# A gated attention and token-MLP block: attention by token halves with pre-added products, a bf16 softmax, weights copied by DMA, and attention summed into the MLP's PSUM

## The chip, the cores and the metric

The kernel runs on one core of one Trainium2 chip, written directly against the engines' instruction queues. Time is the device time of one execution in microseconds (us). A profile is one such execution, and its span runs from the first to the last instruction. Engines: PE (matmul), DVE (vector), ACT (activations), POOL (GpSimd) and SP (which issues DMAs). PSUM is the accumulator memory, which these kernels declare as eight banks of 512 fp32 per partition.

Each execution also lists the mean TensorE clock that was granted, as a share of full speed. The kept traces don't show it for the first 4 to 11 us: their clock records begin that late or are missing, and the profile prints 1.00 where it has none.

## The reference

`x` is 2048 tokens by 512. Two branches are mixed by a gate.

```python
g = sigmoid((x * gate_w).sum(-1))                 # one number per token
# A: 32 heads of 16, each token attends to 8 tokens: itself and those 2, 4, ... 14 before it
q, k, v = split(x @ wqkv)
logits = einsum("bhsd,bhswd->bhsw", q, k[s - 2*w]) * 0.25      # masked where s - 2*w < 0
o = einsum("bhsw,bhswd->bhsd", softmax(logits), v[s - 2*w])
a = o @ wo
# B: an MLP over the tokens
u = gelu(einsum("bsd,sf->bdf", layernorm(x), w1) + b1)         # 2048 -> 1792
b = transpose(einsum("bdf,fs->bds", u, w2) + b2)               # 1792 -> 2048
out = g * a + (1 - g) * b
```

The projections are 192 matmuls of 128x128 by 512, the MLP 448 and `wo` 64. The sliding-window attention has no large matmul: DVE multiplies q with shifted k, and attention weights with shifted v, element by element. PE only sums these products across partitions.

## The kernel before

The kernel names operations with what they read and write. At build time a list scheduler orders each engine's queue, and then every queue runs in order. The parts that the change touches, cut:

```python
# scores: a product of q with 4 shifted k per (half of the window, dl); PE sums each over 4 partitions
for wh in range(2):
    for dl in range(4):
        A("dve", f_qkm(wh, dl, buf), ...)         # tensor_tensor 128x8192 bf16
        A("pe", f_qkr(wh, dl, buf), ...)          # 16 tiled matmuls, 32 output rows each
    A("act", ... LOG[:, 4*wh:4*wh+4] = copy(ps[:, 4:8]) ...)       # fp32
# softmax in fp32: max, subtract, exp, sum, reciprocal, multiply (512 columns)
# 16 DMAs, issued by SP, copy V into the layout of the weights (V3)
# values: product of 4 shifted v with the weights, three adds of 128x2048, then PE sums
for t in range(4):
    for wh in range(2):
        A("dve", f_avm(t, wh, buf), ...)          # tensor_tensor 128x8192 bf16
        ...                                       # ava, avb, avc: 128x2048 adds
        A("pe", f_ws(t, wh, buf), ...)            # 16 tiled matmuls
    A("act", ... OT[:, t] = copy(ps[:, 4:8]) ...)
# MLP, then out = g * (OT @ WO) + T1
for i in range(NST):
    ... 14 matmuls; ACT: T1[:, i] = (1-g) * psum + c2
    A("pe", f_wo(i), ...)                         # 4 matmuls into a bank of their own
    A("dve", ... OUTS = psum * g + T1[:, i] ...)
    sch.dma("sp", ... outv[:, i] = OUTS ...)
```

## Time and profile before

| | before |
|---|---|
| median time of the first three executions | 187.16 us (186.28 to 188.75) |
| span of the profiled execution | 183.8 us |
| PE / DVE / ACT busy | 171.3 / 151.5 / 76.5 us |
| first score product on DVE, first MLP matmul on PE | 25.8, 65.8 us |

The head of the profile's page, and the two lines of its chain of waits. The chain is followed back from the last instruction. The lines give shares of the span by engine, then by source line (L791: second MLP layer; L752: first; L618: score products).

```profile
span 183.8 us, 2564 instructions
...
PE 171.3 (93%) x1071; PEld 80.5 (44%) x1091; DVE 151.5 (82%) x139; ACT 76.5 (42%) x98; POOL 0.9 (0%) x8
...
PE 70%; DVE 22%; ACT 3%; issue 2%; DMA 2%
PE ps L791 26%; PE ps L752 26%; DVE arena L618 18%; PE ps L808 7%; PE ps L584 6%; DVE arena L549 2%; DMA arena<-in_A_x_dram 2%; PE ps L510 2%; PE ps L709 1%; ACT arena L529 1%; ACT L543 1%; PE ps L625 1%; DVE arena L820 0%; ACT arena L765 0
```

PE is busy 93% of the span and makes up 70% of the chain. The costliest groups show each operation with shapes, count, total busy time and mean ns of one:

```profile
L752 PE MATMUL ps<-arena 128*128 128x512 bf16 x219 | 48.5, 379 | 0.4 <-issue 0.2
L584 PE MATMUL ps<-arena 128*128 128x512 bf16 x185 | 44.4, 391 | 2.7 <-ACT arena L529 1.6 <-DVE arena L539 0.5 <-issue 0.3
L701 DVE TENSOR_TENSOR arena<-arena 128x8192 bf16<-128x8192 bf16 x8 | 35.2, 4420 | 0.1
L618 DVE TENSOR_TENSOR arena<-arena 128x8192 bf16<-128x8192 bf16 x8 | 34.9, 4419 | 0.0
...
L625 PE MATMUL ps<-arena 128*32 128x512 bf16 x128 | 8.2, 382 | 0.7 <-DVE arena L618 0.7
...
L709 PE MATMUL ps<-arena 32*32 32x512 bf16 x128 | 3.2, 384 | 0.0
```

A DVE product of 8192 elements takes 4.42 us. The 379 ns of a matmul run from its start to its end, and matmuls overlap. What one costs in a stream comes from the timeline, where a GELU leaves every 3.455 us per 16 matmuls: 0.216 us each.

The timeline (start, duration, engine, line, operation; in brackets the idle time just before and what ended it) fixes three events: the first score products, the first MLP matmul, and DVE's idle time near the end, because only output tiles are left for it.

```profile
25.78 4.42 DVE L618 TENSOR_TENSOR arena<-arena 128x8192 bf16<-128x8192 bf16 x1
...
65.77 1.47 PE L752 MATMUL ps<-arena 128*128 128x512 bf16 x6
...
160.38 3.34 DVE L820 SCALAR_TENSOR_TENSOR arena<-ps,arena 128x512 bf16<-128x512 f32 x4 [7.93 <-PE ps L808]
```

### The profile page before, as it was taken

How to read it: one execution, taken by the hardware profiler on the slowest of the kernel's cores; microseconds unless marked ns; L12 is line 12 of the kernel's file. 1: busy time of each engine (PE TensorE's matmuls, PEld its weight loads, DVE VectorE, ACT ScalarE, POOL GpSimd, SP SyncE). 2: the span in 40 equal slices, each digit the busy share in tenths (PEclk: the TensorE clock that was granted, in tenths of full speed). 3: DMA queues.
4: the chain of work that ended last, by engine and by line, in shares of the span. 5: the costliest groups of instructions: out<-in, count | busy, mean ns of one | idle time of the engine just before them, and what ended most of it. 6: DMA issues, size and time to landing. Idle time of an engine off the chain costs nothing.

```text
span 183.8 us, 2564 instructions
## 1 busy us (share of the span) xinstructions
PE 171.3 (93%) x1071; PEld 80.5 (44%) x1091; DVE 151.5 (82%) x139; ACT 76.5 (42%) x98; POOL 0.9 (0%) x8
## 2 busy tenths in 40 slices
PE   0789999999999989999999999899999999999993
PEld 0455554454564334444434444344444444444441
DVE  0867759999999999699999999999999991056524
ACT  2267686565677373962111251161225226110110
POOL 1000000000000000000000000000000000000000
PEclk9999999999999999999999999999999999999999
DMA  5999990000000079999999200007625742033113
GB/s 181 334 343 262 250 229 5 0 4 2 2 4 0 0 227 173 175 257 214 290 290 291 71 0 0 4 0 200 181 65 157 199 139 65 0 114 114 51 63 114
DMA packets 37870, 23.29 MB, mean 127 GB/s; under 512 B 996, under 2 KB 37860, under 8 KB 37860
## 3 DMA queue, kind: packets, MB, share of 16 engines
q1 hardware_dynamic: 37860, 23.14, 50.6%
q8 instruction: 8, 0.13, 0.3%
q14 instruction: 2, 0.02, 0.0%
HBM read 18.88 MB, written 2.10 MB: 114 GB/s over the span
## 4 chain that ended last, share of the span: by engine, by line
PE 70%; DVE 22%; ACT 3%; issue 2%; DMA 2%
PE ps L791 26%; PE ps L752 26%; DVE arena L618 18%; PE ps L808 7%; PE ps L584 6%; DVE arena L549 2%; DMA arena<-in_A_x_dram 2%; PE ps L510 2%; PE ps L709 1%; ACT arena L529 1%; ACT L543 1%; PE ps L625 1%; DVE arena L820 0%; ACT arena L765 0%; DVE arena L526 0%
## 5 line engine op out<-in xcount | busy, mean ns | idle before, releaser
L791 PE MATMUL ps<-arena 128*128 128x512 bf16 x217 | 49.3, 380 | 1.1 <-ACT arena L765 0.8
L752 PE MATMUL ps<-arena 128*128 128x512 bf16 x219 | 48.5, 379 | 0.4 <-issue 0.2
L584 PE MATMUL ps<-arena 128*128 128x512 bf16 x185 | 44.4, 391 | 2.7 <-ACT arena L529 1.6
L701 DVE TENSOR_TENSOR arena<-arena 128x8192 bf16<-128x8192 bf16 x8 | 35.2, 4420 | 0.1
L618 DVE TENSOR_TENSOR arena<-arena 128x8192 bf16<-128x8192 bf16 x8 | 34.9, 4419 | 0.0
L791 PEld LDWEIGHTS ps<-arena 128*128 128x128 bf16 x224 | 21.5, 98 | 27.6 <-ACT arena L765 1.3
L752 PEld LDWEIGHTS ps<-arena 128*128 128x128 bf16 x224 | 21.6, 98 | 26.8 <-issue 0.8
L584 PEld LDWEIGHTS ps<-arena 128*128 128x128 bf16 x192 | 20.9, 115 | 23.4 <-issue 2.1
L834 ACT ACTIVATE arena<-ps,arena 128x512 bf16<-128x512 f32 x16 | 12.4, 776 | 40.4 <-PE ps L791 40.4
L820 DVE SCALAR_TENSOR_TENSOR arena<-ps,arena 128x512 bf16<-128x512 f32 x16 | 12.0, 751 | 17.2 <-PE ps L808 15.8
L595 ACT ACTIVATE arena<-ps 128x512 bf16<-128x512 f32 x32 | 18.6, 597 | 12.2 <-PE ps L584 12.2
L765 ACT ACTIVATE arena<-ps,arena 128x512 bf16<-128x512 f32 x14 | 9.6, 687 | 27.8 <-PE ps L752 27.7
L808 PE MATMUL ps<-arena 128*128 128x512 bf16 x63 | 14.4, 379 | 0.1
L592 ACT ACTIVATE arena<-ps 128x512 bf16<-128x512 f32 x16 | 9.6, 598 | 8.7 <-PE ps L584 8.7
L539 DVE BATCH_NORM_STATS2 arena<-arena 128x6 f32<-128x512 bf16 x16 | 10.3, 667 | 2.7 <-DMA arena<-in_A_x_dram 2.7
L659 DVE TENSOR_TENSOR arena<-arena 128x512 f32<-128x512 f32 (+2 forms) x10 | 9.0, 905 | 1.7 <-ACT arena L671 1.4
L728 DVE TENSOR_TENSOR arena<-arena 128x2048 bf16<-128x2048 bf16 x8 | 9.8, 1221 | 0.1
L741 ACT ACTIVATE arena<-ps 128x2048 bf16<-128x2048 f32 x4 | 7.5, 1877 | 5.5 <-PE ps L709 5.5
L731 DVE TENSOR_TENSOR arena<-arena 128x2048 bf16<-128x2048 bf16 x8 | 9.7, 1218 | 0.0
L735 DVE TENSOR_TENSOR arena<-arena 128x2048 bf16<-128x2048 bf16 x8 | 9.6, 1221 | 0.1
L808 PEld LDWEIGHTS ps<-arena 128*128 128x128 bf16 x64 | 6.3, 98 | 7.6
L510 PE MATMUL ps<-arena 128*128 128x128 bf16 x64 | 5.2, 245 | 4.5 <-DMA arena<-in_A_x_dram 4.5
(47 smaller groups left out, 70.2 us busy)
## 6 DMA issues: line engine op xcount, KB each, us to landing
arena<-in_B_w_dram SPq DMA_DIRECT2D x7, 1024.0 KB, 10.5
arena<-in_B_w_dram SPq DMA_DIRECT2D x8, 896.0 KB, 5.4
arena<-arena SPq DMA_DIRECT2D x16, 131.5 KB, 6.0
arena<-in_A_x_dram SPq DMA_DIRECT2D x4, 512.0 KB, 6.3
out_dram<-arena SPq DMA_DIRECT2D x16, 128.0 KB, 1.7
arena<-in_A_wqkv_dram SPq DMA_DIRECT2D x3, 512.0 KB, 6.0
arena<-in_A_wo_dram SPq DMA_DIRECT2D x4, 128.0 KB, 5.8
arena<-in_gate_w_dram SPq DMA_DIRECT2D x1, 1.0 KB
```

The lines of the kernel that those rows point to most:

```text
L539: A("dve", (lambda t_: (lambda e: e.bn_stats(out=ST6[:, t_, :], in_=X[:, t_, :])))(t), 0.7, reads=["x%d" % t], writes=["st6_%d" % t], name ...
L584: ins = e.matmul(ps[:, bank, :], lhsT=lhsT, rhs=XT[:, dt, sb * 512:(sb + 1) * 512], start=(dt == 0), stop=(dt == 3))
L595: return lambda e: e.activation(out=dst, in_=ps[:, bank, :], func=AF.Copy)
L618: return lambda e: e.tensor_tensor(out=PBL[buf], in0=in0, in1=in1, op=ALU.mult)
L701: return lambda e: e.tensor_tensor(out=PV[buf], in0=in0, in1=in1, op=ALU.mult)
L728: A("dve", (lambda b_: (lambda e: e.tensor_tensor(out=PV[b_][:, 0, :, :], in0=PV[b_][:, 0, :, :], in1=PV[b_][:, 1, :, :], op=ALU.add)))(bu ...
L731: A("dve", (lambda b_: (lambda e: e.tensor_tensor(out=PV[b_][:, 2, :, :], in0=PV[b_][:, 2, :, :], in1=PV[b_][:, 3, :, :], op=ALU.add)))(bu ...
L752: ins = e.matmul(ps[:, bank, :], lhsT=W1W[:, slot, st, 128 * e_:128 * e_ + 128], rhs=X[:, st, :], start=(st == 0), stop=(st == NST - 1))
L791: ins = e.matmul(ps[:, bank, :], lhsT=W2S[slot][:, ft, 128 * e_:128 * e_ + 128], rhs=UT[:, ft, :], start=(ft == 0), stop=(ft == NFT - 1))
L808: ins = e.matmul(ps[:, WB(i), :], lhsT=OT[:, t, 128 * i:128 * i + 128], rhs=WO[:, t, :], start=(t == 0), stop=(t == 3))
L820: A("dve", (lambda i_: (lambda e: e.scalar_tensor_tensor(out=OUTS[:, i_ % 4, :], in0=ps[:, WB(i_), :], scalar=col(G, i_), in1=T1[:, i_, :] ...
L834: A("act", (lambda i_, bank_: (lambda e: e.activation(out=T1[:, i_, :], in_=ps[:, bank_, :], func=AF.Identity, scale=col(OMG, i_), bias=co ...
```

## The change

The change works on PE, the engine that bounds. It halves the score bursts: all 8 window positions of 1024 tokens form one product, and DVE adds products in pairs before PE sums them, in two bursts of tiled matmuls in all. It abolishes the value bursts, because the weights are copied into V's layout by DMA instead of V into theirs, and the value sum then lies within a partition. It also abolishes the separate output accumulation. The gate is folded into the attention weights (`e^z / sum`, with `1/(1+e^z)` outside), so `OT @ WO` continues in the PSUM of the MLP's tile. The softmax is bf16 at its wide steps. The head is new: small first loads, five warm-up matmuls, three quarters of x transposed by DMA. The core of the diff, cut and condensed:

```diff
-        for wh in range(2):
-            for dl in range(4):
-                A("dve", f_qkm(wh, dl, buf), 4.45, ...)
-                qop = A("pe", f_qkr(wh, dl, buf), 1.15, ...)
+        for h in range(2):
+            for pr in range(2):
+                for k_ in range(2):
+                    A("dve", tt(PB[bb[k_]], <q, 8x broadcast>, <k, 8 shifts>, ALU.mult), 4.42, ..., name="qk%d_%d")
+                A("dve", tt(PB[bb[0]], PB[bb[0]], PB[bb[1]], ALU.add), 4.42, ..., name="qa%d_%d")
+            A("pe", f_sum(h, b0, b1, h == 0), ...)            # 32 tiled matmuls; the gate's 16 with h == 0
+            ... zclip, zexp: e^z by ACT; softmax of LOG[h], ATT[h] in bf16
+            A("dve", tt(RB, RS, EB[:, h * UT_:(h + 1) * UT_], ALU.mult), ...)     # weights times e^z
+            for c in range(4):
+                for dhi in range(4):
+                    prev = sch.dma("pool", <AVW[h] <- ATT[h], 32 partitions to every fourth>, 131072, ...)
...
-                A("pe", f_ws(t, wh, buf), 0.03 * 16 * len(AV_SLOTS) + 0.1, ...)
-            A("act", <OT from PSUM>, 1.95, ...)
+        for u in range(8):
+            A("dve", tt(pv, <V, 8 shifts>, <AVW>, ALU.mult), 4.42, ..., name="avm%d" % u)
+            A("dve", tt(pv[:, 0:4], pv[:, 0:4], pv[:, 4:8], ALU.add), 2.28, ..., name="ava%d" % u)
+            A("dve", tt(pv[:, 0:2], pv[:, 0:2], pv[:, 2:4], ALU.add), 1.22, ..., name="avb%d" % u)
+            A("dve", tt(OT[:, u], pv[:, 0], pv[:, 1], ALU.add), 0.68, ..., name="avc%d" % u)
...
-            A("dve", <OUTS = psum * g + T1>, 0.75, ...)
+        def finish_tile(i):
+            PE(f_wo(i, bank, 0, D), 0.87, ["ot%d" % (i // 2), "wo"], ["b%d" % bank], "wo%d" % i)   # same bank as the MLP
+            A("act", act(OUTS[:, i % 4, :], ps[:, bank, :], AF.Identity, scale=col(OMG, i), bias=col(C2, i)), 0.78, ...)
...
+        for i in range(L):                                    # L = 15, LAG = 3
+            ... 14 MLP matmuls of tile i
+            if i >= LAG:
+                finish_tile(i - LAG)
+        for i in range(L - LAG, L):
+            finish_tile(i)
+        ... tile 15 in two halves of 256 columns
```

Tensor-tensor operations are all recorded at one helper line of the new kernel (L439), and activations at another (L442).

## The prediction

> **What bounds it now.** PE. The busy table has PE 171.3 of 183.8 us (93%), DVE 151.5, ACT 76.5; the chain of waits is 70% PE. In the timeline a GELU tile leaves every 3.455 us per 16 matmuls, 0.216 us each, so the 704 full matmuls (projections 192, MLP 448, output projection 64) need 152 us. The rest of PE, from the groups: x transposes 5.2, eight score bursts 8.2, eight value bursts 3.2, gate 1.7. The head adds more: first matmul at 4.5 us, the first eight projection matmuls at 0.43 us each (half speed), the MLP begins only at 65.8. DVE makes its first score product at 25.9 us and is idle most of the time after 152.4.
>
> **Removed from PE.** 48 of 64 transposes (x comes transposed by DMA) and about half of the cold start (five warm-up matmuls, smaller first loads): 5 us. Score bursts: 128 tiled matmuls become 64, about 4 us less. Value bursts: 3.2 us. Gate: about 1 us less. Most of the head's idle time: 3 to 4 us. The MLP should begin near 52 us.
>
> **Added or moved.** DVE makes the same eight 8192-element products for scores and eight for values (4.42 us each, spaced 4.335), plus four pre-adds of that size (17.3 us) and longer value trees (4.1 us of adds per unit instead of 3.6 per half round, 4 us more in all). The softmax falls from about 28 us to 15: bf16 at 1.14 us per 2048 elements instead of 2.29, but the fp32 sums and the reciprocal (3.35 us per 512) keep their rate. The V-layout copy is replaced by 32 copies of weights, 128 KB each, issued by POOL; the old 16 took 6.0 us to land. The final DVE combine (12 us) and the copy out of PSUM (ACT 7.5 us) vanish, because attention accumulates in the MLP's PSUM.
>
> **Sum.** First score product when q and k of the first 1024 tokens are out, about 16.5 us. DVE then has some 143 us: products and pre-adds 87, value trees 32, softmax 15, normalisation 8. It ends near 160 if nothing stalls. PE: head 11, projections 38, sums and gate 5, MLP 97, output projection 14, gaps 1: 166. The last output tiles need the last value unit only near 161, so PE still bounds and DVE has about 3 us of slack. Tail 2.5 us (before: 2.2 from the last DVE instruction to the end). Span about 169.5; the time exceeds the span by 3.4 as before: **173 us**, 168 to 180 in 8 of 10. Chances: faster 0.94, same 0.04, slower 0.02.
>
> **What would show it.** The MLP's first matmul at 50 to 55 us; DVE's first product at 15 to 18; PE busy 158 to 163; the last value add at 157 to 164; DVE gaps below 5 us in total after 17 us.
>
> **What would make it wrong.** DMA transposes: the Trainium skill, "DMA: Bandwidth & Descriptors", Latency and other measured facts, gives 261 GB/s for one kernel; 0.5 MB would land in 2 us (estimate; nothing here shows it). If three of them hold the queue, the head grows. Copies issued by POOL: the skill, "SBUF — State Buffer", Who interferes with whom, says tensor_tensor blocks only GpSimd's reads and thinks descriptor writing unaffected; if descriptor writing is blocked by DVE, value products wait, and with 3 us of slack every further microsecond reaches the end. GELU may not overwrite the transposed x before the gate's burst; if the first scores come late, PE stands still at the MLP's start.

## More of the kernel before

Next come the stages by busy time: start and end, length, busy us of each engine with instruction counts, then granted clock, DMA share and GB/s. I cut at the first matmul of each MLP layer.

```profile
core 0: us, PE busy (x) PEld busy (x) DVE busy (x) ACT busy (x) POOL busy (x), PEclk, DMA share, GB/s
0.00:65.77 65.77, 57.80 (x444) 30.20 (x452) 54.93 (x69) 37.90 (x58) 0.86 (x8) 1.00 0.43 114
65.77:116.07 50.30, 49.15 (x256) 21.85 (x257) 48.29 (x34) 20.83 (x21) 0.00 (x0) 1.00 0.85 180
116.07:183.80 67.73, 64.36 (x376) 28.48 (x384) 48.25 (x37) 17.74 (x19) 0.00 (x0) 1.00 0.33 99
```

## The result, and the profile after

The changed kernel takes **177.19 us** (median of 4, 175.21 to 178.73, the last slow) against 187.45 us for the kernel before on the same chip. The ratio is 0.945 (95% interval 0.937 to 0.953). Six more executions in a later set gave 178.11 us and a ratio of 0.9525 (0.947 to 0.958). A ratio here is fast runs of one kernel over fast runs of the other in the same set, so it is not quite the ratio of the medians quoted. Executions over 1.5% slower than the fastest of the same kernel are left out of the means. The output is correct. The measured time lies in the stated range, 4 to 5 us above the point.

The first profile of the changed kernel is of its fastest execution, 175.21 us. The head of its page and its chain:

```profile
span 173.1 us, 2087 instructions
...
PE 162.4 (94%) x846; PEld 78.8 (46%) x846; DVE 154.4 (89%) x114; ACT 70.2 (41%) x96; POOL 18.3 (11%) x54
...
DVE 71%; PE 11%; issue 7%; DMA 4%; ACT 3%; POOL 1%; SPq 1%; DVEq 0%
DVE arena L439 63%; PE ps L610 3%; DVE arena L664 3%; DVE arena L650 3%; ACT arena L442 2%; PE ps L797 2%; DMA arena<-in_A_x_dram 2%; DMA arena<-arena 2%; DVE arena L717 2%; PE ps L788 2%; PE ps L565 1%; PE ps L762 1%; PE ps L681 1%; POOL a
```

PE lost 9 us of work (171.3 to 162.4), yet the chain is now 71% DVE. The same three stages, cut at the first matmul of each MLP layer:

```profile
0.00:50.69 50.69, 46.22 (x232) 25.25 (x233) 40.84 (x41) 32.12 (x54) 1.40 (x22) 1.00 0.68 177
50.69:104.84 54.15, 53.49 (x308) 23.86 (x309) 52.62 (x44) 25.11 (x25) 8.52 (x16) 1.00 0.68 192
104.84:173.10 68.26, 62.68 (x307) 29.69 (x305) 60.92 (x31) 12.93 (x17) 8.37 (x16) 1.00 0.36 110
```

| stage (span) | before | after, first profile | after, second profile |
|---|---|---|---|
| to the first MLP matmul | 65.8 | 50.7 | 52.4 |
| first MLP layer | 50.3 | 54.1 | 54.1 |
| second layer, output, end | 67.7 | 68.3 | 70.1 |
| sum | 183.8 | 173.1 | 176.6 |

The whole gain comes before the MLP: 13 to 15 us. The first layer grew because both score bursts and the gate's now fall into it. The last stage should have shrunk by the value bursts that fell into it (2.3 of the 3.2 us) and did not. Its timeline says why (in the order of PE's first projection, DVE's first product, the MLP's first matmuls, then the end):

```profile
10.81 17.46 PE L610 MATMUL ps<-arena 128*128 128x512 bf16 x80 [0.69 <-ACT arena L442]
...
16.84 13.22 DVE L439 TENSOR_TENSOR arena<-arena 128x8192 bf16<-128x8192 bf16 x3 [0.80 <-ACT arena L442]
...
50.69 1.89 PE L762 MATMUL ps<-arena 128*128 128x512 bf16 x8 [1.12 <-ACT arena L442]
53.23 1.90 PE L762 MATMUL ps<-arena 128*128 128x512 bf16 x8 [0.65 <-DVE arena L664]
...
152.94 12.55 DVE L439 TENSOR_TENSOR arena<-arena 128x8192 bf16<-128x8192 bf16 x7
...
159.66 1.03 PE L797 MATMUL ps<-arena 128*128 128x512 bf16 x4
...
163.69 2.90 PE L797 MATMUL ps<-arena 128*128 128x512 bf16 x12 [3.00 <-DVE arena L439]
```

DVE makes its last value add at 165.5 us (152.94 + 12.55). PE is through with what it may do at 160.7, waits 3.00 us, and only then runs the last three output projections, followed by the last tile's MLP. What ends the wait is the last add of unit 6 (at 163.6 us), which tiles 12 and 13 need; unit 7's, the last, comes 1.9 us later, while PE works on those two.

The second profile, of the changed kernel run again, is of a more typical execution. The end by windows, with the same columns as above (the last line is a part of the one before it), and its first PE piece after the wait:

```profile
161.00:165.60 4.60, 1.40 (x8) 0.43 (x6) 4.57 (x5) 0.78 (x1) 0.00 (x0) 1.00 0.08 29
165.60:174.00 8.40, 8.38 (x48) 5.08 (x48) 1.77 (x2) 2.90 (x4) 0.00 (x0) 0.80 0.17 55
...
166.80:170.20 3.40, 3.40 (x12) 1.34 (x10) 0.60 (x1) 1.84 (x3) 0.00 (x0) 0.50 0.23 77
```

```profile
165.60 4.15 PE L797 MATMUL ps<-arena 128*128 128x512 bf16 x12 [3.20 <-DVE arena L439]
```

Here the wait was 3.20 us, and the clock granted behind it is 0.80 in the mean. The mean hides a step: for 1.2 us after the wait the clock is still 1.00, then 0.50 for 3.4 us (matmuls 0.427 us apart in place of 0.216), then 1.00 again. Half speed for 3.4 us costs 1.7 us. The same 12 matmuls that took 2.90 us took 4.15. From the end of the wait to DVE's reading of PE's last result is 8.41 us (165.60 to 174.01), against 6.87 us (163.69 to 170.56) in the first profile. Of the ten executions of this kernel, nine have a mean clock of 0.99 and take 176.95 to 178.88 us. The tenth, at 1.00, takes 175.21. The two profiles' spans differ by 3.5 us: 1.9 are there before the first projection (10.81 and 12.75 us), 1.5 arise behind the wait.

### The profile page after: what moved, and what is told of

Its sections match the earlier page's. It is cut to its first block, busy times and chain, and to the rows that moved or that the text cites. A ratio compares the mean times of both kernels' runs of the same rounds, so it can differ in the third digit from the quotient of the medians.

```text
span 173.1 us, 2087 instructions
## 1 busy us (share of the span) xinstructions
PE 162.4 (94%) x846; PEld 78.8 (46%) x846; DVE 154.4 (89%) x114; ACT 70.2 (41%) x96; POOL 18.3 (11%) x54
## 4 chain that ended last, share of the span: by engine, by line
DVE 71%; PE 11%; issue 7%; DMA 4%; ACT 3%; POOL 1%; SPq 1%; DVEq 0%
DVE arena L439 63%; PE ps L610 3%; DVE arena L664 3%; DVE arena L650 3%; ACT arena L442 2%; PE ps L797 2%; DMA arena<-in_A_x_dram 2%; DMA arena<-arena 2%; DVE arena L717 2%; PE ps L788 2%; PE ps L565 1%; PE ps L762 1%; PE ps L681 1%; POOL arena L729 1%; SPq L476 1%
## 5 line engine op out<-in xcount | busy, mean ns | idle before, releaser
L439 DVE TENSOR_TENSOR arena<-arena 128x2048 bf16<-128x2048 bf16 (+9 forms) x68 | 133.4, 2002 | 2.7 <-DMA arena<-arena 0.9
L762 PE MATMUL ps<-arena 128*128 128x512 bf16 x224 | 49.2, 379 | 1.8 <-ACT arena L442 1.1
L442 ACT ACTIVATE arena<-ps,arena 128x512 bf16<-128x512 f32 (+1 forms) x30 | 21.6, 728 | 71.9 <-PE ps L797 51.1
L788 PE MATMUL ps<-arena 128*128 128x512 bf16 (+1 forms) x238 | 50.7, 366 | 0.0
L442 ACT ACTIVATE arena<-ps 128x512 bf16<-128x512 f32 (+3 forms) x53 | 33.4, 645 | 26.1 <-PE ps L610 10.4
L610 PE MATMUL ps<-arena 128*128 128x512 bf16 x176 | 38.6, 379 | 0.8 <-ACT arena L442 0.7
L788 PEld LDWEIGHTS ps<-arena 128*128 128x128 bf16 x238 | 23.3, 98 | 25.3
L762 PEld LDWEIGHTS ps<-arena 128*128 128x128 bf16 x224 | 21.6, 98 | 28.8 <-ACT arena L442 1.6
L610 PEld LDWEIGHTS ps<-arena 128*128 128x128 bf16 x176 | 19.7, 114 | 19.0 <-ACT arena L442 1.5
L729 POOL DMA_DIRECT2D arena<-arena x32 | 16.9, 531 | 95.7 <-DVE arena L439 95.7
L797 PE MATMUL ps<-arena 128*128 128x512 bf16 (+1 forms) x68 | 16.4, 367 | 3.0 <-DVE arena L439 3.0
L797 PEld LDWEIGHTS ps<-arena 128*128 128x128 bf16 x68 | 6.5, 98 | 10.6 <-DVE arena L439 3.9
L565 PE MATMUL ps<-arena 128*128 128x256 bf16 x32 | 4.0, 278 | 1.5 <-DVE arena L555 0.8
L664 DVE TENSOR_SCALAR arena<-arena 128x512 bf16<-128x512 bf16 x16 | 5.3, 409 | 0.0
L442 ACT ACTIVATE arena<-arena 128x2048 bf16<-128x2048 bf16 (+3 forms) x5 | 4.9, 984 | 0.1
L565 PEld LDWEIGHTS ps<-arena 128*128 128x128 bf16 x32 | 3.4, 115 | 2.0 <-DVE arena L555 1.9
L526 PE MATMUL ps<-arena 128*128 128x512 bf16 x5 | 2.3, 629 | 1.1 <-POOL arena L445 1.1
```

The source lines that it names most:

```text
L439: return lambda e: e.tensor_tensor(out=o_, in0=a_, in1=b_, op=op_)
L442: return lambda e: e.activation(out=o_, in_=i_, func=f_, **kw)
L565: ins = e.matmul(ps[:, dl, hb * 256:hb * 256 + 256], lhsT=sub(WQKV, dt * 3 * D + dl, [(4, 128)]), rhs=XT[:, dt, hb * 256:hb * 256 + 256], ...
L610: ins = e.matmul(ps[:, bank, :], lhsT=sub(WQKV, dt * 3 * D + tn * D + dl, [(4, 128)]), rhs=XT[:, dt, sb * 512:(sb + 1) * 512], start=(dt = ...
L664: A("dve", (lambda t_: lambda e: e.tensor_scalar(out=X[:, t_, :], in0=X[:, t_, :], scalar1=col(RSTD, t_), scalar2=col(NMR, t_), op0=ALU.mu ...
L729: prev = sch.dma("pool", (lambda d_, s_: lambda e: e.dma_start(d_, s_))(dst, src), 131072, ds, issue=1.0, reads=["att%d" % h], writes=["av ...
```

## Experiments

Two theories. **A**: DVE's queue, from its first product to its last add, now ends last, and what PE must do behind it is exposed. **A1** is an addition to it: PE's wait also costs clock, so it costs more than its length. **B**: PE's own work still bounds, as the prediction said, and the wait at the end is an accident of the profile.

| run | change | median us | ratio to before (95%) | clock |
|---|---|---|---|---|
| e0_after_again | none | 178.11 | 0.9525 (0.947–0.958) | 0.99 in 6 of 6 |
| e1_tail | PE's end reordered | 172.96 | 0.9270 (0.922–0.932) | 1.00 |
| e2_head | projections reordered | 176.77 | 0.9431 (0.937–0.949) | 1.00 in 2 of 6 |
| e3_both | both | 172.87 | 0.9237 (0.919–0.929) | 1.00 |
| e5_fill | useless PE work in the wait | 175.99 | 0.9440 (0.940–0.949) | 1.00 in 6 of 6 |
| e4_dve_plus | one product twice | 182.07 | 0.9765 (0.970–0.983) | 0.98 to 0.99 |
| e7_before_dve_plus | the same on the kernel before | 187.01 | 1.0039 (0.997–1.011) | 1.00 |
| e11_banks | e3 and other banks | **171.52** | **0.9194** (0.915–0.924) | 1.00 |
| e6_no_preadd | e1, no pre-adds | 174.24 | 0.9349 (0.931–0.939) | 1.00 |
| e8_no_warm | e1, no warm-up | 173.37 | 0.9290 (0.926–0.932) | 1.00 |
| e9_pe_transpose | e1, PE transposes | 180.78 | 0.9676 (0.964–0.971) | 0.98 to 0.99 |
| e10_sp_copies | e1, copies by SP | 172.79 | 0.9248 (0.922–0.928) | 1.00 |

All outputs were correct. Clocks are rounded to two decimals. The first four runs shared one chip and set of runs of the kernel before; so did the next four, and the last four. Where runs of different sets are compared I use the ratios; 0.01 of ratio is 1.87 us.

### The changed kernel again, and its end reordered

> The changed kernel unchanged, as the measure for the others of this set: about 177 us, span of the profiled run 173 to 176, DVE without a gap over 1 us from 17 to 165 us, PE standing still about 3 us near 161 for the last value units.

Measured: 178.11 us; the profiled span of 176.6 us lies just above the expected 173 to 176, and PE's wait was 3.20 us, ending at 165.6.

e1_tail lets PE do the last tile's MLP before the output projections that wait:

```diff
-        for i in range(L - LAG, L):
-            finish_tile(i)
         for hf, (c0, c1) in enumerate(((0, 256), (256, 512))):
             ... MLP matmuls of tile 15, columns c0:c1
-            PE(f_wo(L, bank, c0, c1), ...)
+        for i in range(L - LAG, L):
+            finish_tile(i)
+        for hf, (c0, c1) in enumerate(((0, 256), (256, 512))):
+            PE(f_wo(L, lastb[hf], c0, c1), ...)
```

> Only the order of PE's last work differs: the MLP matmuls of the last output tile come before the output projections of tiles 12 to 14, so that PE has 3 us of work that needs no attention while DVE ends. Theory A (DVE's queue ends last, and what stands behind its last add is 5 us of PE work, of which 3 need not stand there): about 3 us less, 170 of span where the changed kernel has 173. Theory B (PE's own work bounds, the 3 us wait is an accident of the profile): within 1 us.

Measured: 172.96 against 178.11 us, 5.2 us less (4.8 by the ratios), and the clock is 1.00 in every execution. Theory B expected under 1 us, and A alone expected 3. The end of the timeline:

```profile
152.78 12.55 DVE L439 TENSOR_TENSOR arena<-arena 128x8192 bf16<-128x8192 bf16 x7
...
161.09 3.22 PE L788 MATMUL ps<-arena 128*128 128x256 bf16 x28
...
164.36 3.41 PE L797 MATMUL ps<-arena 128*128 128x512 bf16 x19
```

The 28 half-width MLP matmuls fill the time in which DVE ends (165.3 us), and PE goes on without a gap. The chain of the same run is PE's again:

```profile
PE 71%; DVE 22%; DMA 3%; issue 1%; SPq 1%; ACT 1%; DVEq 0%
```

One caution: the build-time scheduler also moved some of DVE's instructions. Their stretch was hardly shorter for it (147.9 us from first product to last add, 148.7 before), so at most 0.9 of the 5.2 us can come from that.

### Is the clock a cost of its own?

e5_fill keeps every wait, and in place of the pause PE runs 14 matmuls on a constant into a free bank. They are declared to the scheduler as taking no time, so the order of all else stays.

```diff
+        def f_fill(e):
+            for _ in range(14):
+                ins = e.matmul(ps[:, 3, :], lhsT=ONES, rhs=ONES4, start=True, stop=True)
+            return ins
+        PE(f_fill, 0.01, ["ones"], ["b3"], "fill")
         for i in range(L - LAG, L):
             finish_tile(i)
```

> The changed kernel, every wait kept, with 14 useless matmuls (3.0 us of PE work) put where PE stands still for the last value units. Theory A1 (the pause costs twice: its own 3 us, and a lower granted clock for the PE work behind it in most executions): the clock stays at 1.00 in every execution, PE's end after the last value add is 5.0 us and not 6.6, so 1.5 to 2 us FASTER than the changed kernel though PE does more: 175 to 176 us. Theory A2 (the lower clock has another cause, such as the length of the load before it): the clock is 0.99 as before, 177 to 178 us. Theory B (PE bounds): 3 us slower.

Measured: 175.99 us, so PE does 3 us more work and the kernel is 2.1 us faster by the medians (1.6 us by the ratios, with intervals that just overlap; against the changed kernel's first set, 0.945, the ratio is the same). The clock is 1.00 in six of six executions. Firmer than the whole time is how long DVE, after its last add, waits for PE's last result: 5.06 us with the filler, 5.06 in the first profile (clock 1.00), 6.61 in the second. A1 holds; A2 and B fall. The filler, then the work that waited:

```profile
161.23 3.18 PE L824 MATMUL ps<-arena 128*128 128x512 bf16 x14
...
164.52 2.90 PE L797 MATMUL ps<-arena 128*128 128x512 bf16 x12
```

The 12 matmuls behind the filler take 2.90 us again. So the pause cost its 3 us and, in most executions, a further 1.5 to 2 us of slow matmuls. Together they make up most of the 4.8 to 5.2 us that e1_tail regained.

### Which engine bounds: the same dose on both kernels

One value product is written twice, 4.34 us more on DVE, in the changed kernel (unit 4) and in the kernel before (round 4):

```diff
+            if u == 4:
+                A("dve", tt(pv, <the same operands>, ALU.mult), 4.42, ..., name="avmx%d" % u)
```

> The changed kernel with one value product of unit 4 done twice (4.34 us more on DVE). Theory A (DVE bounds from its first product on): 4.3 us more, 182 us, the pause of PE near its end or ends grows by as much. Theory B (PE bounds with slack for DVE): under 1.5 us more.

> The kernel before with one value product done twice (4.34 us more on DVE), the same dose as in the run on the changed kernel. If the kernel before is bound by PE, as the prediction says, the ratio stays at 1.00 (under 0.7 us more). If DVE sat on its path too, 4.3 us more.

Measured: the changed kernel goes from a ratio of 0.9525 to 0.9765, which is 4.5 us. The kernel before stays at 1.004 (0.997 to 1.011), so at most 2.0 of the 4.34 us show there. So in its value rounds DVE had time to spare before, and after the change it had none. The dose says nothing of the head of the kernel before: from 25.9 to 64.8 us its chain of waits runs mostly through DVE, and no run tests that part. In the changed kernel the pause grew, three waits of 1.7 us in all came before it, and the matmuls behind it got slower still (5.30 us for the same twelve):

```profile
168.99 5.30 PE L800 MATMUL ps<-arena 128*128 128x512 bf16 x12 [5.80 <-DVE arena L439]
```

### An earlier start for DVE

```diff
         for dl in range(4):
             proj(0, dl, 1)
-        for dl in range(4):
             proj(1, dl, 0)
             proj(1, dl, 1)
```

> Only the order of the projections differs: q and k of one column group after another, so that DVE's first score product can start after 3 projections in place of 6 (2.6 us earlier, near 14.2 us). Theory A (DVE bounds from its first product to its last add): 2.5 us less. Theory B (PE bounds): no change in time, the first product earlier all the same.

Measured: a miss. Only 1.3 us less by the medians (1.8 by the ratios, with intervals that overlap), and part of that is luck: two of the six executions kept the clock at 1.00 (175.1 us). The four others took 176.7 to 177.9. DVE's queue shows where the 2.5 us went. First the changed kernel, then e2_head: layer-norm statistics before the products, the products, and the first instructions behind them.

```profile
12.59 3.66 DVE L650 BATCH_NORM_STATS2 arena<-arena 128x6 f32<-128x512 bf16 x6 [2.77 <-DMA arena<-in_A_x_dram]
18.54 22.09 DVE L439 TENSOR_TENSOR arena<-arena 128x8192 bf16<-128x8192 bf16 x5 [2.30 <-ACT arena L442]
40.55 3.65 DVE L650 BATCH_NORM_STATS2 arena<-arena 128x6 f32<-128x512 bf16 x6
```

```profile
13.09 1.88 DVE L649 BATCH_NORM_STATS2 arena<-arena 128x6 f32<-128x512 bf16 x3 [4.04 <-DMA arena<-in_A_x_dram]
15.19 22.09 DVE L439 TENSOR_TENSOR arena<-arena 128x8192 bf16<-128x8192 bf16 x5 [0.21 <-ACT arena L442]
37.19 5.43 DVE L649 BATCH_NORM_STATS2 arena<-arena 128x6 f32<-128x512 bf16 x9
```

DVE does begin earlier. Counted from PE's first projection (12.75 us in the one profile, 11.98 in the other), the first product moved from 5.8 to 3.2 us. But the time before the products was not idle. Six statistics instructions ran in it; now three do, and the others (1.8 us) stand behind the first five products. Measured from PE's first projection, DVE's last add came only 0.6 us earlier (154.1 against 154.7).

> Both reorderings. Theory A: DVE ends 2.6 us earlier and PE no longer waits for it; then PE bounds, whose work and other gaps leave 170.5 less the 3 us wait = 167.5 for its last matmul: span near 170, 3 to 4 us less than the changed kernel, so not the sum of the two (5.5). Theory B: no change.

Measured: 172.87 us with both reorderings, no better by the medians than the end alone (172.96); by the ratios 0.6 us less, within the intervals. (It is 5.2 us less than the changed kernel, where 3 to 4 were expected: the expectation left the clock out.) Once the end is reordered, an earlier DVE no longer helps by more than that. PE leads the chain here (71%), but narrowly: in the profile of e10_sp_copies, whose PE has the same order, the chain is 70% DVE.

### The best version: PE need not wait for a bank

The first four projections go to banks 4 to 7, which are free by then, so that PE does not wait for q to be copied out of banks 0 to 3.

```diff
         def proj(tn, dl, sb):
-            bank = bank_()
+            nproj[0] += 1
+            bank = 3 + nproj[0] if nproj[0] <= 4 else bank_()
```

> Both reorderings, and the first four projections go to PSUM banks 4 to 7 so that PE needn't wait 0.93 us for the first q tile to be copied out. If PE bounds once its last pause is gone: 0.9 us less than with both reorderings alone, 172.0 us. If the start of DVE's products or the loads bound: no change.

Measured: **171.52 us**, a ratio of 0.9194 against 0.9237 for e3_both, so 0.8 us less where 0.9 was expected. The wait of 0.93 us before the projections is gone from the profile; the gain in time is not shown, as the intervals overlap widely. It beats both kernels: 8% less than before, and 3.5% less than the changed kernel by the ratios.

### What the parts are worth, on the kernel with the reordered end

e6_no_preadd takes the pre-adds out. PE sums all four products of a half in two bursts, with three buffers in rotation:

```diff
-                A("dve", tt(PB[bb[0]], PB[bb[0]], PB[bb[1]], ALU.add), 4.42, ...)
-            A("pe", f_sum(h, b0, b1, h == 0), ...)
+                A("pe", f_sum(h, pr, b0, b1, wg), ...)        # start with the first pair, stop with the second
```

> On the kernel with the reordered end (172.96 us): the pre-adds are taken out, PE sums all four products of a half in two bursts of 32 tiled matmuls (128 in all, as in the kernel before). DVE does 17.3 us less, PE 64 tiled matmuls more, 1.9 us per 32 in the traces. If PE bounds that kernel, as theory A says of it: 3.8 us more, 176.8 us. If DVE still bounds it: faster.

Measured: 174.24 us, a ratio of 0.9349 against 0.9270: 1.5 us more, not 3.8, with intervals that just overlap. (Against e10_sp_copies, of the same set, it is 1.9 us more, clear of noise.) PE did do the extra work (165.7 us busy against 161.4). But the holes that PE has at the MLP's start in e1_tail are gone. These are e1_tail's waits of PE (who waited for whom: us in total, times, longest):

```profile
PE ps L762 <- ACT arena L442: 1.1, 1, 1.1
...
PE ps L762 <- DVE arena L664: 0.7, 1, 0.7
...
PE ps L762 <- issue: 0.3, 2, 0.2
```

None of these 2.1 us exists in e6_no_preadd. Its DVE is far ahead and at the end waits 17.7 us for PE:

```profile
DVE arena L836 <- PE ps L797: 17.7, 1, 17.7
```

So the pre-adds pay, but little: 17.3 us of DVE buy 1.5 us. In the changed kernel as it was made, where DVE ended last, they probably cost more than they brought. That is argued from these runs, not run.

e8_no_warm deletes the warm-up:

```diff
-        PE(f_warm(5), 2.1, ["ones"], ["b7"], "warm")
```

> On the kernel with the reordered end: the five warm-up matmuls are taken out. If they are why the first projections run at full speed (1.95 us per 16 half-width matmuls, against 0.43 us per full one in the kernel before), the head is 1.5 to 3.5 us longer and so is the time: about 175.5 us. If the wait for the loads sets the head: under 0.7 us.

Measured: 173.37 us, a ratio of 0.9290 against 0.9270, so 0.4 us and within noise. The first group of 16 half-width matmuls runs at half speed without it, and the second at full speed. Below, e8_no_warm, then the first group of e0_after_again, which has the warm-up:

```profile
4.98 3.57 PE L564 MATMUL ps<-arena 128*128 128x256 bf16 x16 [0.91 <-DMA arena<-in_A_wqkv_dram]
...
9.93 1.94 PE L564 MATMUL ps<-arena 128*128 128x256 bf16 x16 [0.52 <-DVE arena L554]
```

```profile
4.93 3.58 PE L565 MATMUL ps<-arena 128*128 128x256 bf16 x16 [0.69 <-DMA arena<-in_A_wqkv_dram]
```

So the warm-up does not always work. In the eleven profiles that have it, the first group took 1.9 to 2.3 us in six, 3.0 in e5_fill, and 3.6 in four (e0_after_again, e3_both, e10_sp_copies, e11_banks). The first projection starts at 12.55 us here; with the warm-up it starts at 10.81 to 11.98 where that group was not at 3.6 us, and at 12.37 to 12.95 where it was (e9_pe_transpose, which transposes in between, left out). So the slow group goes with a head longer by about 1.2 us; its own start, which the loads set, lies between 4.75 and 5.7 us in all of them. Why the warm-up works in one execution and not in another is not shown.

e9_pe_transpose returns all of x to PE's transposes:

```diff
-        ld_xt(1)
+        ld_x(4, 4)
...
+        do_tx(1)                      # 8 transposes to PSUM, copied out half by DVE, half by ACT
         for dl in range(4):
             proj(0, dl, 1)
```

> On the kernel with the reordered end: x is transposed by PE again throughout (48 more transposes in six groups of 0.61 us, 12 more copies out of PSUM) and the three DMA transposes are gone. If PE's work bounds: 3.7 us more, 176.7 us. If the head's loads bound (they move 1.5 MB less): less than that, down to none.

Measured: 180.78 us, a ratio of 0.9676 against 0.9270: 7.6 us more, twice the expectation. The 48 transposes take 3.8 us in three groups (1.06, 1.06, 1.65), as expected. The rest looks like the mechanism of e5_fill in another place; this is read from one profile, and no run separates it. The copies out of PSUM stand in DVE's queue behind 4.4 us products, so PE stands still:

```profile
24.07 1.06 PE L541 MATMUL ps<-arena 128*128 128x128 bf16 x16
28.57 1.65 PE L541 MATMUL ps<-arena 128*128 128x128 bf16 x16 [3.44 <-DVE arena L552]
```

The clock granted in the window that follows is 0.69 in the mean (0.50 from 28.9 to 32.3 us):

```profile
28.57:34.00 5.43, 5.43 (x30) 3.19 (x31) 5.43 (x5) 2.46 (x5) 0.00 (x0) 0.69 0.00 0
```

e10_sp_copies issues the weight copies from SP:

```diff
-                    prev = sch.dma("pool", ..., issue=1.0, ...)
+                    prev = sch.dma("sp", ..., issue=0.6, ...)
```

> On the kernel with the reordered end: the 32 copies of weights are issued by SP in place of POOL. If POOL's descriptor writing were held up by DVE (the prediction's worry), copies land sooner and the time falls; the profile shows only one wait of 0.9 us of DVE for them, so I expect no change (within 0.7 us), with SP's own queue of weight loads perhaps held up behind them.

Measured: 172.79 us, a ratio of 0.9248 against 0.9270: the same within noise. POOL's issuing was not a cost that shows.

## Why the prediction was right, and where it was wrong

Right in substance: faster, within the range, and with the gain in the head, as forecast. Wrong about the end, where the step named below failed; that the time still came within 4 to 5 us is in part luck (see the offset). Point by point:

- **PE bounds the kernel before.** Shown by e7_before_dve_plus for the value rounds: 4.34 us of DVE added nothing beyond the noise. For the head, where the gain arose, it is not tested.
- **The head is where the gain lies.** Predicted: first MLP matmul near 52 us and first product at 16.5. Measured: 50.7 and 16.8 (first profile), 52.4 and 18.5 (second). PE busy was predicted at 158 to 163 and was 162.4 and 164.8, and the first product at 15 to 18: the second profile is outside both.
- **Its parts were not all sized right.** "About half of the cold start (five warm-up matmuls, smaller first loads)": the warm-up is worth 0.4 us within noise (e8). The DMA transposes are worth 7.6 us in e9's form, about half of that, by the reading above, because the copies of PE's transposes collide with DVE's products. The "four microseconds less" of score bursts are 1.5 net in e6. No run takes the parts one by one from the kernel before, so how they add up to the 13 to 15 us is not shown.
- **"PE still bounds and DVE has about 3 us of slack" is the step that failed.** DVE's last add was predicted near 160 and came at 165.5. From first product to last add DVE needed 148.7 us, not 143, with only 0.9 us of waiting in it. Counted from each instruction's start to the next one's, products and pre-adds took 87.1 us (87 predicted), value trees 32.8 (32), softmax 16.7 (15), normalisation 8.9 (8). The rest had been left out: eleven small layer-norm, mask and gate instructions and three copies and casts (2.3 us) and the waiting. Part of the excess in trees and softmax is that an instruction that reads its predecessor's result starts 0.03 us after its end, while independent ones start 0.08 us before it; in 34 places of the stretch the next instruction starts after the end.
- **What a miss of the slack costs was not in the sum.** I wrote that every further microsecond of DVE reaches the end. It does (e4_dve_plus), but the wait it makes on PE, 3.2 us and more in four profiles, also lowers the clock behind it, for another 1.5 to 2 us (e5_fill). For the second profile, with PE's end at 174.0 us against my 166, the account is: a later head 1.8 (its first group of matmuls was at half speed, 3.58 us against 2.01 in the first profile), the wait 3.2, the slow matmuls 1.5, gaps at the MLP's start 0.9 above the allowance. That is 7.4 of 8.0.
- **"The time exceeds the span by 3.4 as before" was wrong and hid part of the miss.** I subtracted a fast profile's span (183.8) from a median of other executions. Later executions of the kernel before have spans of 183.5 to 186.8, and the difference is 1.7 to 2.2 us in all. The span was missed by 7 us in the typical execution (176.6 against 169.5), the time only by 5.
- **POOL and the DMA transposes as risks.** The Trainium skill, "SBUF — State Buffer", section "Who interferes with whom", has tensor_tensor block only GpSimd's reads, with descriptor writing inferred to be unaffected. This agrees: the 32 issues took 0.53 us each in the median while DVE ran its instructions, DVE waited 0.9 us for a copy, and SP in POOL's place changed nothing (e10). The three DMA transposes landed 5.2 to 8.8 us after issue with the queue in front of them. No run here isolates their rate, so the prediction's estimate of 2 us stays untested.

The Trainium skill, "TensorE: Matmul & The Clock Gate", section "Why this matters for your kernels", says to avoid PE-idle gaps above about 3 us between bursts of matmuls. I had not used it, and it is the missing term: in these profiles a pause of 3.00 us kept the clock, and pauses of 3.20, 3.44 (twice) and 5.80 us lost it. Five pauses give no sharp border. Two of e2_head's six executions kept the clock, and their pauses were not profiled. Nor need length be all: in the clock records every stretch between two changes is a whole multiple of 3.41 us (3.41, 6.83, 23.89, 157.01, 160.43, 163.84), and the half speed began 1.2, 0.6 and 0.3 us after PE had resumed (e0_after_again, e2_head, e9_pe_transpose) and 0.9 us before it in e4_dve_plus. Where a pause lies on that grid may count as well; no run separates the two.

What stays open: when the clock first rises in the head, and whether undoing only some of the pre-adds would be better than e11_banks. The slow matmuls of e8_no_warm's head (3.57 us) stand beside a printed clock of 1.00, but the trace's first clock record, at 1.00, comes at 9.33 us, behind them. It comes at 9.80 in e0_after_again and at 11.24 in the kernel before, also just behind slow matmuls, and at 4.26 in e4_dve_plus, where the first group took 1.9 us. So the head's slowness looks like the half speed of the end.

## What to carry to other kernels

When a change relieves the bounding engine by loading the next one, compute when the second engine's last result comes and what the first must still do after it, then put work that doesn't need that result last in line before the wait; here that order alone was worth 5 us of 178. A wait of 3.2 us on PE cost more than itself, because matmuls behind it ran at half speed for 3.4 us; useless matmuls in the pause kept the clock, which saved 1.5 us behind it. Before calling an engine's early time idle, look at what its queue does there: moving its main work earlier only pushes that back.

## What the Trainium skill lacked or had wrong

- "TensorE: Matmul & The Clock Gate" gives both "~3µs" and "~3.4µs" for the idle gap that loses the clock. Here 3.20 us already lost it, and 3.00 us kept it in one profile. The page does not say that the pause can be filled with useless matmuls at a profit: DVE's last wait for PE is 5.06 us with them and 6.61 without.
- The same page, section "Back-to-back issue gap", gives about 131 ns per matmul of 512 columns for a sustained stream of weight loads and matmuls, and calls 216 ns the isolated figure. The streams here run at 216 ns (3.455 us per 16).
- "VectorE: DVE Perf Modes", section "The DRAIN you can't avoid", reports a test in which a semaphore after each instruction cost nothing extra, and gives no size for how much sooner an unheld one starts. Here independent tensor-tensor instructions start 0.08 us before their predecessor's end and dependent ones 0.03 us after it: 0.1 us for each dependent step.
- No page that I read warns that a small PSUM copy for PE, queued on DVE behind 4.4 us instructions, can cost PE 3.4 us and then its clock (a granted 0.69 in the window that follows).
